# Two linear-attention branches under a gate: x^T phi(k) partial products carried on in PSUM, and some min-and-epsilon steps on GpSimd

## The chip, the cores and the metric

The kernel runs on one core of one Trainium2 chip. The metric is the device time of one execution in microseconds (us), from runs on the chip; the median of the runs shown is compared. "PE" is TensorE, "PEld" its weight loads, "DVE" VectorE, "ACT" ScalarE, "POOL" GpSimd.

## The reference

Two branches, A and B, work on the same input x (2048 rows of 640, bf16) with their own weights, and a sigmoid gate mixes their outputs:

```
phi(t) = where(t > 0, t + 1, exp(t)) + 1e-6
q, k, v = x @ wqkv                       # 32 heads of 20
kv  = phi(k)^T v        z = sum over rows of phi(k)
o   = phi(q) kv / (phi(q) z + 1e-6)
branch = o @ wo
out = g * A(x) + (1 - g) * B(x),   g = sigmoid(sum(x * gate_w))
```

## The kernel before, in words

The kernel never makes v. It uses phi(k)^T v = (x^T phi(k))^T wv, so that the long product over 2048 rows is G = x^T phi(k), 640 x 640, and everything behind it is small until the output product. The order of the work on TensorE, for branch A and then for branch B:

- **k chunks** (`k_chunk`, matmuls L205). x is cut into 16 chunks of 128 rows. A chunk is ten matmuls of 320 columns into one PSUM slot of two banks; there are four slots, `ps0` to `ps3`, used in turn. `phi` then makes phi(k) from the slot in three steps: ScalarE writes e = exp(slot) to SBUF (L195), VectorE makes e = min(e, 1) + epsilon (L198), and VectorE makes pk = max(slot + 1 + epsilon, e) (L202), which reads the slot a last time and so frees it. The tile `e` has three buffers.
- **q units** (`q_unit`, `q_block`, L254 and L265): the same for phi(q), transposed, with 1024 columns for a `phi`.
- **z** (`z_rows` L370, `z_pass` L385): column sums of phi(k), and `zsel`, with which the denominators are made.
- **G, last fifth** (`g_pass`, L288): the fifth column block of x against all of pk, into slot 1; ScalarE copies it out (L285).
- **G, the other four fifths** (`g_strassen`, products `g_prod` L315): a 2 x 2 block product by Strassen's method in Winograd's form, seven products of 16 matmuls of 320 columns in place of eight. The sums of blocks that it needs are made earlier by VectorE (`x_sum`, `k_sum`, by `add_rows` L454). The accumulators are `even` (slot 0) and `odd` (slot 1). The first product, P1, is needed in several results: ScalarE copies it to an SBUF tile `p1` in fp32 (L337), and VectorE adds `p1` to three later products while it takes them out of PSUM (`add`, L332).
- **the denominators** (`rec_pass` L435: 40 matmuls L169 into slot 2, then twice an L444 and a reciprocal L449 on VectorE), **their spreading** (`norm_spread`: eight matmuls L491 into slots 2 and 3, two ScalarE copies L496 to `R`), and **scaling** (`scale` L504, five VectorE products of 2048 columns on phi(q)). These stand between the products of `g_strassen`.

In branch B, `p_diff` (four L454 of 1280 columns) stands behind k chunks 3, 6, 9 and 12. After B's `g_strassen` the output stage begins: `kvt_mm` (L396), `kvt_mask` (L403) and so on, and then the output product, again by Strassen's method, in pairs of row blocks.

The order on each engine is the order of the program text wherever `tc.manual_schedule()` holds: in the first chunks of A, and from A's chunk 14 to the end. Between them (A's chunks 4 to 13 and five q pieces) the framework orders the work itself. `hc` is 8.

Of the kernel before, what the change touches and what calls it, by code (L numbers as in the profile page):

```python
# [12 lines left out]
ALU = mybir.AluOpType  # L13
# [8 lines left out]
HF = D // 2  # L22
# [3 lines left out]
EPS = 1e-6  # L26
# [5 lines left out]
def kernel(  # L32
# [11 lines left out]
    nc = tc.nc  # L44
# [19 lines left out]
    def ps(name, slot=None):  # L64

        return ps_raw(name, slot).bitcast(FP32).rearrange("p (b n) -> p b n", b=2)
# [3 lines left out]
    pk = persist.tile([P, ST, D], BF16, name="pk")  # L70
# [14 lines left out]
    hc, ic = ST // 2, 2 * P  # L85

    def flat(t, pattern, inner, at=0):
        n = hc * inner
        return t[:].rearrange(pattern)[:, at * n:(at + 1) * n].rearrange("p (i n) -> p i n", i=hc)

    S3 = persist.tile([P, 3, hc, ic], BF16, name="S3")
    SX = {k: S3[:, k - 1] for k in (1, 2, 3)}
    SX[4] = flat(M[1], "p c d -> p (c d)", ic)
    TK = [{k: flat(pqT[1], "p c s -> p (c s)", HF, k - 1) for k in (1, 2, 3, 4)},
          {k: flat(xT, "p c s -> p (c s)", HF, k - 2) for k in (2, 3, 4)}]
# [33 lines left out]
    for n in range(1, NB):  # L129
        for c in range(DT):  # L130
            nc.sync.dma_start_transpose(
                out=xT[:, c, n * HB:(n + 1) * HB], in_=x2[n * HB:(n + 1) * HB, c * P:(c + 1) * P]
# [4 lines left out]
    for r in range(4):  # L137
# [3 lines left out]
        out=spread[:].rearrange("p (h t) -> p h t", t=TW), in_=I4[:, :, None].to_broadcast([P, H, TW])  # L141
    )
    nc.gpsimd.memset(maskE[:], 1.0)
    for sign, base in ((1, 0), (-1, Dh - 1)):
        nc.gpsimd.affine_select(
            out=maskE[:], in_=maskE[:], pattern=[[-sign * Dh, KG // Dh], [0, Dh]],
# [3 lines left out]
    for r in range(4):  # L150
        rows = slice(32 * r, 32 * r + 32)
        for sign, base in ((1, 0), (-1, Dh - 1)):
            nc.gpsimd.affine_select(
                out=E4[rows], in_=E4[rows], pattern=[[sign, D]],
# [9 lines left out]
    def by_group(dst, lhsT, src, h):  # L164

        for c in range(DT):
            for j in range(4):
                r0 = h * 2 * HB + j * RB
                nc.tensor.matmul(  # L169
                    dst[32 * j:32 * j + 32, :], lhsT=lhsT[:, c, :], rhs=src[:, c, r0:r0 + RB],  # L170
                    start=(c == 0), stop=(c == DT - 1), tile_position=(0, 32 * j),
                )
# [16 lines left out]
        for lo, hi in zip(cuts, cuts[1:]):  # L189
            copy(out=xT[:, lo:hi, i * P:(i + 1) * P], in_=src[:, lo:hi])  # L190

    def phi(dst, src, n, lifted=False):

        e = work.tile([P, 2, n], BF16, tag="e", name="e", bufs=3)
        nc.scalar.activation(out=e[:], in_=src, func=ACT.Exp)  # L195
        if lifted:
            nc.scalar.activation(out=dst, in_=src, func=ACT.Identity, bias=lift[:])
        nc.vector.tensor_scalar(e[:], e[:], 1.0, EPS, op0=ALU.min, op1=ALU.add)  # L198
        if lifted:
            nc.vector.tensor_tensor(out=dst, in0=dst, in1=e[:], op=ALU.max)  # L200
            return
        nc.vector.scalar_tensor_tensor(out=dst, in0=src, scalar=1.0 + EPS, in1=e[:], op0=ALU.add, op1=ALU.max)  # L202
# [5 lines left out]
        )  # L208

    def k_done(b, i, pt):  # L210
        phi(pk[:, i, :].rearrange("p (b n) -> p b n", b=2), pt[:, :, 0:HF], HF)

    def k_chunk(b, i, slot=None):
        pt = ps(f"k{'AB'[b]}", slot)
        for hf in range(2):
            for c in range(DT):
                k_mm(b, i, c, pt, hf)
        k_done(b, i, pt)
# [74 lines left out]
    def x_sum(k):  # L293

        x11, x21 = [xn[:, 0:hc, n:n + ic] for n in (0, ic)]
        x12, x22 = [xn[:, hc:ST, n:n + ic] for n in (0, ic)]
        a, b, op = {
            1: (x21, x22, ALU.add), 2: (SX[1], x11, ALU.subtract),
            3: (x11, x21, ALU.subtract), 4: (x12, SX[2], ALU.subtract),
        }[k]  # L300
        add_rows(SX[k], a, b, op)

    def k_sum(b, k):

        b11, b12 = [pk[:, 0:hc, n * HF:(n + 1) * HF] for n in range(2)]
        b21, b22 = [pk[:, hc:ST, n * HF:(n + 1) * HF] for n in range(2)]
        t = TK[b]
        left, right = {1: lambda: (b12, b11), 2: lambda: (b22, t[1]), 3: lambda: (b22, b12), 4: lambda: (b21, t[2])}[k]()
        add_rows(t[k], left, right, ALU.subtract)

    def g_prod(pt, left, right, first):

        for i in range(hc):
            for n in range(2):
                nc.tensor.matmul(  # L315
                    pt[:, n, 0:HF], lhsT=left[:, i, n * P:(n + 1) * P], rhs=right[:, i, :],
                    start=(first and i == 0), stop=(i == hc - 1), skip_group_check=not first,
                )

    def g_strassen(b, norm):  # L320

        x11, x12 = [xn[:, k:k + hc, 0:ic] for k in (0, hc)]
        x22 = xn[:, hc:ST, ic:2 * ic]
        b11 = pk[:, 0:hc, 0:HF]
        b21, b22 = [pk[:, hc:ST, n * HF:(n + 1) * HF] for n in range(2)]
        lo, hi = GT

        def temp(name):
            return work.tile([P, 2, HF], FP32, tag="osb", name=name, bufs=3)

        def add(dst, pt, sb):
            nc.vector.tensor_tensor(out=dst, in0=pt[:, :, 0:HF], in1=sb[:], op=ALU.add)  # L332

        even, odd = ps("gs0", 0), ps("gs1", 1)
        g_prod(even, x11, b11, True)
        p1 = temp("p1")
        nc.scalar.copy(out=p1[:], in_=even[:, :, 0:HF])  # L337
        g_prod(odd, SX[2], TK[b][2], True)
        u2 = temp("u2")
        add(u2[:], odd, p1)  # L340
        k_sum(b, 4)
        norm()
        g_prod(even, x12, b21, False)
        nc.scalar.copy(out=lo[:, 0:2, :], in_=even[:, :, 0:HF])
        scale(b, 0)
        if b == 0:
            x_sum(4)
        g_prod(odd, SX[3], TK[b][3], False)
        u3 = temp("u3")
        add(u3[:], odd, p1)  # L350
        scale(b, 1)
        scale(b, 2)
        even = ps("gs0", 0)
        g_prod(even, SX[1], TK[b][1], True)
        add(hi[:, 2:4, :], even, u3)
        scale(b, 3)
        g_prod(odd, x22, TK[b][4], False)
        add(lo[:, 2:4, :], odd, p1)
        scale(b, 4)
        g_prod(even, SX[4], b22, False)  # L360
        for n in range(2):
            nc.vector.tensor_tensor(out=hi[:, n, :], in0=even[:, n, 0:HF], in1=u2[:, n], op=ALU.add)
# [72 lines left out]
    def rec_pass(b, zsel, slot):  # L435

        pt = ps(f"den{'AB'[b]}", slot)
        for h in range(2):
            by_group(pt[:, 0, h * RB:(h + 1) * RB], zsel, pqT[b], h)
        rts = []  # L440
        for h in range(2):
            part = slice(h * RB, (h + 1) * RB)
            d1 = work.tile([P, RB], FP32, tag="d1", name="d1")
            nc.vector.scalar_tensor_tensor(  # L444
                out=d1[:], in0=pt[:, 0, part], scalar=EPS, in1=ge[b][:, part], op0=ALU.add, op1=ALU.mult
            )
            rT = work.tile([P, RB], BF16, tag="rT", name="rT")
            with nc.allow_low_precision(reason="a fp32 reciprocal, stored as the bf16 that multiplies bf16"):
                nc.vector.reciprocal(out=rT[:], in_=d1[:])  # L449
            rts.append(rT)  # L450
        return rts

    def add_rows(dst, a, b, op):
        nc.vector.tensor_tensor(out=dst, in0=a, in1=b, op=op)  # L454
# [30 lines left out]
    def norm_spread(b, rts, slots):  # L485

        pts = [ps(f"ex{'AB'[b]}", s) for s in slots]
        for h in range(2):
            for j in range(4):
                rows = slice(32 * j, 32 * j + 32)  # L490
                nc.tensor.matmul(  # L491
                    pts[j // 2][:, j % 2, h * RB:(h + 1) * RB], lhsT=spread[rows, :], rhs=rts[h][rows, :],
                    start=True, stop=True,
                )
        for jj in range(2):
            nc.scalar.copy(  # L496
                out=R[:, :, 2 * jj:2 * jj + 2, :].rearrange("p h j n -> p j h n"),
                in_=pts[jj][:].rearrange("p j (h n) -> p j h n", n=RB),
            )

    def scale(b, m):

        rec = R[:].rearrange("p h j n -> p (h j n)")
        nc.vector.tensor_tensor(out=pqT[b][:, m, :], in0=pqT[b][:, m, :], in1=rec, op=ALU.mult)  # L504
# [127 lines left out]
    def g_all(b, zsel):  # L632

        g_pass(b, DT - 1, 1)
        k_sum(b, 3)
        rts = rec_pass(b, zsel, 2)
        g_strassen(b, lambda: norm_spread(b, rts, (2, 3)))


    with tc.manual_schedule():  # L640
# [12 lines left out]
    for n in range(1, NB):  # L653
        nc.sync.dma_start(
            out=xn[:, n * CB:(n + 1) * CB, :], in_=x2[n * HB:(n + 1) * HB, :].rearrange("(q p) d -> p q d", p=P)
# [11 lines left out]
    with tc.manual_schedule():  # L667
# [5 lines left out]
        zsel = q_pass(0, [(m, 1) for m in range(DT)])  # L673
        wq[1] = load_w(1, "q", nc.sync)
        g_all(0, zsel)

        turn[0] = 3
# [10 lines left out]
        zsel = q_pass(1, [(m, h) for h in range(2) for m in range(DT)])  # L688
# [53 lines left out]
        for i in range(1, half):  # L742
            p, after = pairs[i], pairs[i + 1] if i + 1 < half else None
# [53 lines left out]
```

## Time and profile before

| | |
|---|---|
| median of 2 runs | 192.75 us (192.75 to 192.76) |
| profiled execution, span from first to last instruction | 190.2 us |
| the difference of the two | 2.55 us |
| mean granted TensorE clock | 0.997 |
| PE busy in 27 to 38 us (A's k chunks 8 to 15) | 11.00 of 11.00 us |
| PE busy in 74.2 to 96.2 us (B's k chunks) | 22.00 of 22.00 us; DVE 18.67, ACT 10.56, POOL 0.00 |
| PE busy in 122.6 to 137 us (B's G) | 14.40 of 14.40 us; DVE 13.16 |
| PE busy in 137 to 147 us (end of B's G, begin of the output) | 9.85 of 10.00 us; DVE 8.56 |
| POOL, whole span | 8.5 us busy, all before 10 us |

The profile is of one execution; its own time is given only as the span. The span does not hold what lies before the first and after the last instruction; the difference to the median stands in the table. A line of the timeline reads: start, duration, engine, source line, operation, output and inputs with their shapes, and how many instructions were merged. A line of the chain of waits reads: start, duration, engine, tile, source line.

### The profile page before, as it was taken

The page shows a single profiled execution, that of the slowest core. Times are in us where ns is not written, and L with a number is a line of the kernel's source. Part 1 is how long each engine was busy: PE and PEld are TensorE (multiplying, and loading weights), DVE is VectorE, ACT ScalarE, POOL GpSimd, SP SyncE. Part 2 cuts the span into 40 slices and gives each one's busy share as a digit, 9 for nine tenths or more (in the row PEclk, how much of TensorE's full clock was granted, in tenths as well). Part 3 has the DMA queues.
Part 4 walks back from the last instruction along what each step waited for, and adds up shares of the span by engine and source line. Part 5 has one row for each costly group of instructions (what it writes and reads, how often), then busy time and mean ns, then how long its engine had stood idle before and what let it go on. Part 6 is the DMA issues. An engine that isn't in the chain of part 4 may idle for free.

```text
span 190.2 us, 3774 instructions
## 1 busy us (share of the span) xinstructions
PE 185.8 (98%) x1575; PEld 125.4 (66%) x1575; DVE 151.6 (80%) x242; ACT 70.0 (37%) x98; POOL 8.5 (4%) x23
## 2 busy tenths in 40 slices
PE   8999999999999999999999999999999999999992
PEld 3766657765576777777765555576777776777772
DVE  1498779898989997799976785899797989787553
ACT  2155445455941502355543654511501611111110
POOL 8900000000000000000000000000000000000000
PEclk9999999999999999999999999999999999999998
DMA  6965459970050000500000007000000002312112
GB/s 194 332 147 89 101 117 374 281 201 3 2 172 3 0 0 0 150 26 0 3 0 0 3 2 172 3 0 0 3 0 0 3 0 97 113 69 72 69 69 71
DMA packets 18880, 14.00 MB, mean 74 GB/s; under 512 B 9392, under 2 KB 18864, under 8 KB 18864
## 3 DMA queue, kind: packets, MB, share of 16 engines
q1 hardware_dynamic: 18288, 13.11, 25.0%
q10 hardware_dynamic: 576, 0.66, 1.0%
q8 instruction: 12, 0.20, 0.5%
q14 instruction: 4, 0.03, 0.1%
HBM read 9.18 MB, written 2.62 MB: 62 GB/s over the span
## 4 chain that ended last, share of the span: by engine, by line
PE 92%; DVE 5%; issue 1%; ACT 0%; DVEq 0%; ACTq 0%
PE gs L315 13%; PE qB L254 12%; PE kA L205 12%; PE kB L205 11%; PE qA L254 7%; PE ox L515 5%; PE oy L515 5%; PE oz L515 5%; PE qA L265 5%; PE ow L515 2%; PE gB L288 2%; PE gA L288 2%; DVE pqTB L504 2%; PE warm L162 2%; PE mA L429 2%; DVE osb L520 1%
## 5 line engine op out<-in xcount | busy, mean ns | idle before, releaser
L205 PEld LDWEIGHTS <-xT 128*128 128x128 bf16 x320 | 31.0, 98 | 12.4 <-DVE xT L190 0.2
L198 DVE TENSOR_SCALAR e<-e 128x640 bf16<-128x640 bf16 (+1 forms) x52 | 18.9, 363 | 11.6 <-ACT e L195 11.1
L205 PE MATMUL kA<-wkA,xT 128*128 128x320 bf16 x160 | 22.6, 299 | 0.0
L254 PE MATMUL qB<-xT,wqB 128*128 128x512 bf16 x100 | 22.5, 380 | 0.0
L205 PE MATMUL kB<-wkB,xT 128*128 128x320 bf16 x160 | 22.1, 299 | 0.0
L195 ACT ACTIVATE e<-kB 128x640 bf16<-128x640 f32 x16 | 11.3, 704 | 20.7 <-PE kB L205 19.4
L254 PEld LDWEIGHTS <-wqB 128*128 128x128 bf16 x100 | 11.4, 118 | 9.7 <-issue 0.7
L195 ACT ACTIVATE e<-kA 128x640 bf16<-128x640 f32 x16 | 11.1, 704 | 12.5 <-PE kA L205 12.5
L195 ACT ACTIVATE e<-qB 128x1024 bf16<-128x1024 f32 x10 | 10.2, 1023 | 12.7 <-PE qB L254 12.7
L202 DVE SCALAR_TENSOR_TENSOR pk<-kA,e 128x640 bf16<-128x640 f32 x16 | 13.2, 825 | 1.7
L202 DVE SCALAR_TENSOR_TENSOR pk<-kB,e 128x640 bf16<-128x640 f32 x16 | 13.2, 824 | 1.7
L195 ACT ACTIVATE e<-qA 128x1024 bf16<-128x1024 f32 x10 | 10.2, 1023 | 10.6 <-PE qA L254 5.2
L254 PE MATMUL qA<-xT,wqA 128*128 128x512 bf16 x60 | 13.6, 380 | 0.0
L202 DVE SCALAR_TENSOR_TENSOR pqTB<-qB,e 128x1024 bf16<-128x1024 f32 x10 | 12.2, 1224 | 1.0
L315 PEld LDWEIGHTS <-xn 128*128 128x128 bf16 x96 | 9.1, 98 | 4.2 <-issue 0.8
L315 PEld LDWEIGHTS <-S 128*128 128x128 bf16 x96 | 9.4, 98 | 3.6
L558 ACT COPY u<-ox 128x320 f32<-128x320 f32 x8 | 3.4, 425 | 21.9 <-PE ox L515 21.9
L254 PEld LDWEIGHTS <-wqA 128*128 128x128 bf16 x60 | 6.9, 118 | 5.6 <-issue 0.3
L515 PEld LDWEIGHTS <-xT 128*128 128x128 bf16 x85 | 8.0, 98 | 3.1 <-DVE xT L454 0.2
L515 PEld LDWEIGHTS <-pqTA 128*128 128x128 bf16 x85 | 7.9, 98 | 2.9 <-issue 0.2
L515 PEld LDWEIGHTS <-pqTB 128*128 128x128 bf16 x80 | 7.8, 98 | 3.0
L542 ACT COPY p1s<-ox 128x320 f32<-128x320 f32 x8 | 3.4, 426 | 16.8 <-PE ox L515 16.8
(120 smaller groups left out, 288.1 us busy)
## 6 DMA issues: line engine op xcount, KB each, us to landing
out_dram<-osb SPq DMA_DIRECT2D x14, 160.0 KB, 1.8
xn<-in_A_x_dram SPq DMA_DIRECT2D x3, 640.0 KB, 6.3
wqA<-in_A_wqkv_dram SPq DMA_DIRECT2D x1, 800.0 KB, 5.5
wvA<-in_A_wqkv_dram SPq DMA_DIRECT2D x1, 800.0 KB, 9.6
woA<-in_A_wo_dram SPq DMA_DIRECT2D x1, 800.0 KB, 12.6
wkB<-in_B_wqkv_dram SPq DMA_DIRECT2D x1, 800.0 KB, 4.7
wqB<-in_B_wqkv_dram SPq DMA_DIRECT2D x1, 800.0 KB, 4.8
wvB<-in_B_wqkv_dram SPq DMA_DIRECT2D x1, 800.0 KB, 4.6
```

Of the source, the lines that this page charges most:

```text
L162: nc.tensor.matmul(warm[:, 0, :], lhsT=one_l, rhs=one_r, start=True, stop=True)
L195: nc.scalar.activation(out=e[:], in_=src, func=ACT.Exp)
L198: nc.vector.tensor_scalar(e[:], e[:], 1.0, EPS, op0=ALU.min, op1=ALU.add)
L202: nc.vector.scalar_tensor_tensor(out=dst, in0=src, scalar=1.0 + EPS, in1=e[:], op0=ALU.add, op1=ALU.max)
L205: nc.tensor.matmul(pt[:, hf, 0:HF], lhsT=xT[:, c, i * P:(i + 1) * P], rhs=wk[b][:, c, hf * HF:(hf + 1) * HF], start=(c == 0), stop=(c == D ...
L254: nc.tensor.matmul(pt[:, u, :], lhsT=mixed(wq[b][:, c, :], m), rhs=xT[:, c, n * HB:(n + 1) * HB], start=(c == 0), stop=(c == DT - 1),)
L265: nc.tensor.matmul(pt[:, u, :], lhsT=mixed(wq[b][:, c, :], m + u), rhs=xT[:, c, n * HB:(n + 1) * HB], start=(c == 0), stop=(c == DT - 1),)
L288: nc.tensor.matmul(pt[:, hf, 0:HF], lhsT=xn[:, i, c * P:(c + 1) * P], rhs=pk[:, i, hf * HF:(hf + 1) * HF], start=(i == 0), stop=(i == ST - 1),
L315: nc.tensor.matmul(pt[:, n, 0:HF], lhsT=left[:, i, n * P:(n + 1) * P], rhs=right[:, i, :], start=(first and i == 0), stop=(i == hc - 1), s ...
L429: nc.tensor.matmul(dst[32 * g:32 * g + 32, :], lhsT=mixed(heads, c), rhs=wo_sb[b][:KG, 2 * g + k, hf * HF:(hf + 1) * HF], start=(k == 0), ...
L504: nc.vector.tensor_tensor(out=pqT[b][:, m, :], in0=pqT[b][:, m, :], in1=rec, op=ALU.mult)
L515: nc.tensor.matmul(dst, lhsT=left[:, c, r0:r0 + P], rhs=right[:, c, :], start=(first and c == 0), stop=(c == DT - 1), skip_group_check=not ...
```

## The change

It has two parts.

In `g_strassen`, P1's copy no longer goes to SBUF: ScalarE copies it from `even` to `odd` in PSUM, and the second product is accumulated onto it. `odd` then holds P1 + P2, later P1 + P2 + P4, and later that plus P6, so that three results come out by a plain ScalarE copy in place of a VectorE addition with `p1`. `rec_pass` moves from ahead of `g_strassen` to between the first product and the second; `norm_spread` moves from behind the second product to behind the third (in branch A behind `x_sum(4)` in the text, which is VectorE's); the five `scale` calls move back by some places.

In `phi` the step e = min(e, 1) + epsilon can be given to another engine. `k_done` gives it to GpSimd for chunks with i % 3 == 1, in branch A only those beyond `hc`: A's chunks 10 and 13, B's chunks 1, 4, 7, 10 and 13, seven in all.

```diff
-    def phi(dst, src, n, lifted=False):
+    def phi(dst, src, n, lifted=False, eng=None):
...
-        nc.vector.tensor_scalar(e[:], e[:], 1.0, EPS, op0=ALU.min, op1=ALU.add)
+        (eng or nc.vector).tensor_scalar(e[:], e[:], 1.0, EPS, op0=ALU.min, op1=ALU.add)
...
     def k_done(b, i, pt):
-        phi(pk[:, i, :].rearrange("p (b n) -> p b n", b=2), pt[:, :, 0:HF], HF)
+        eng = nc.gpsimd if i % 3 == 1 and (b == 1 or i > hc) else None
+        phi(pk[:, i, :].rearrange("p (b n) -> p b n", b=2), pt[:, :, 0:HF], HF, eng=eng)
...
         even, odd = ps("gs0", 0), ps("gs1", 1)
         g_prod(even, x11, b11, True)
-        p1 = temp("p1")
-        nc.scalar.copy(out=p1[:], in_=even[:, :, 0:HF])
-        g_prod(odd, SX[2], TK[b][2], True)
+        nc.scalar.copy(out=odd[:, :, 0:HF], in_=even[:, :, 0:HF])
+        rts = rec_pass(b, zsel, 2)
+        g_prod(odd, SX[2], TK[b][2], False)
         u2 = temp("u2")
-        add(u2[:], odd, p1)
+        nc.scalar.copy(out=u2[:], in_=odd[:, :, 0:HF])
         k_sum(b, 4)
-        norm()
         g_prod(even, x12, b21, False)
         nc.scalar.copy(out=lo[:, 0:2, :], in_=even[:, :, 0:HF])
-        scale(b, 0)
         if b == 0:
             x_sum(4)
+        norm_spread(b, rts, (2, 3))
         g_prod(odd, SX[3], TK[b][3], False)
         u3 = temp("u3")
-        add(u3[:], odd, p1)
+        nc.scalar.copy(out=u3[:], in_=odd[:, :, 0:HF])
+        scale(b, 0)
         scale(b, 1)
-        scale(b, 2)
         even = ps("gs0", 0)
         g_prod(even, SX[1], TK[b][1], True)
         add(hi[:, 2:4, :], even, u3)
+        scale(b, 2)
         scale(b, 3)
         g_prod(odd, x22, TK[b][4], False)
-        add(lo[:, 2:4, :], odd, p1)
+        nc.scalar.copy(out=lo[:, 2:4, :], in_=odd[:, :, 0:HF])
         scale(b, 4)
         g_prod(even, SX[4], b22, False)
```

`g_all` calls `g_strassen(b, zsel)` and no longer `rec_pass`. Below, P1 to P7 are the products in the order of the text.

More of the change, by code (lines that the diff above doesn't have):

```diff
@@ L318, in g_prod, with g_strassen @@
                 )
-    def g_strassen(b, norm):
+    def g_strassen(b, zsel):
         x11, x12 = [xn[:, k:k + hc, 0:ic] for k in (0, hc)]
@@ L635, in g_all @@
         k_sum(b, 3)
-        rts = rec_pass(b, zsel, 2)
-        g_strassen(b, lambda: norm_spread(b, rts, (2, 3)))
+        g_strassen(b, zsel)
     with tc.manual_schedule():
```

## The prediction

> **What bounds the kernel now.** I read the page's busy times and slices first, then the chain of waits, then the timeline of the two stages that the change touches.
>
> ```profile
> PE 185.8 (98%) x1575; PEld 125.4 (66%) x1575; DVE 151.6 (80%) x242; ACT 70.0 (37%) x98; POOL 8.5 (4%) x23
> PE   8999999999999999999999999999999999999992
> PEclk9999999999999999999999999999999999999998
> ```
>
> TensorE is at work in every slice but the first and the last, at full clock; the change leaves the number and size of its matmuls as they are. So the question of a few us is not what VectorE saves, but where TensorE waits for anybody. The chain of waits goes along TensorE from 0.84 to 137.40 us and from 145.50 to 184.08; in between it leaves it once:
>
> ```profile
> 132.60 0.33 PE exB L491 x8
> 132.93 4.47 PE gs L315 x32
> ...
> 143.12 1.13 DVE pqTB L504
> 144.25 0.80 DVE GT L362 x2
> 145.05 0.41 DVE KVT L403
> 145.45 0.04 issue
> 145.50 0.93 PE mid L396 x20
> ```
>
> VectorE is late with the scaling and the additions at the end of branch B's G, and TensorE waits for the mask of L403. How long, the timeline shows: the matmuls before it (L515, from 144.50, five at 0.136) leave room from 145.18, so the wait is 145.50 - 145.18 = 0.32 us. The waits for single engines show TensorE waiting otherwise only 0.8 us at the start. Nothing else in the part that changes can be won.
>
> **The change, part 1: G, branch B** (A has the same order, one `x_sum` of 1.22 more on VectorE, and no reader that is pressed behind it; its second group of k chunks follows).
>
> ```profile
> 128.09 2.35 PE L315 MATMUL gs<-pk,xn 128*128 128x320 bf16 x16
> 130.47 0.69 ACT L337 COPY p<-gs 128x640 f32<-128x640 f32 x1 [2.68 <-PE gs L315]
> 133.02 1.93 ACT L496 CAST R<-exB 128x1024 bf16<-128x1024 f32 x2 [1.86 <-PE exB L491]
> 134.98 1.23 DVE L504 TENSOR_TENSOR pqTB<-pqTB,R 128x2048 bf16<-128x2048 bf16 x1
> 141.57 2.34 PE L315 MATMUL gs<-pk,MB 128*128 128x320 bf16 x16
> 144.17 0.88 DVE L362 TENSOR_TENSOR GT<-gs,u 128x320 bf16<-128x320 f32 x2
> ```
>
> The rows to use: a product takes 2.18 us of TensorE (its record is 0.16 longer, as the ends overlap), the denominators' 40 matmuls 1.21, the spreading 0.33, an ACT copy of 640 columns 0.69, `R` 1.93, a scaling 1.12 from start to start, an addition (L332) 0.74.
>
> Removed from VectorE: three additions per branch, 6 in all, 6 x 0.74 = 4.4 us, of which 2.2 in B. Added to ScalarE: u2, u3 and half of lo, 3 x 0.69 per branch; it is idle for most of this stage. The copy of P1 stays one copy of 0.69.
>
> *The new wait.* P2 must wait for the copy from `even` to `odd`. TensorE now goes from L288 straight to P1 (126.88 to a record end of 129.23), the copy runs from 129.26, 0.03 behind as before, to 129.95, and the 40 matmuls of the denominators, which TensorE does in the meantime, end near 130.28. The copy has 1.0 us and needs 0.7, so the wait costs nothing. No row shows ScalarE writing PSUM. The bounds: the 0.43 that it takes for 320 columns (a gain of nothing, as the cover is larger anyway) and 1.38, twice the row, which would cost 1.38 - 1.0 = 0.4 per branch, 0.8 in all. I take 0.69: same engine, same source, same 640 columns.
>
> *The denominators.* They end at 130.34 in place of 128.15. VectorE needs 4.27 us from there to its second reciprocal (128.20 to 132.48 before); TensorE before had P1 and P2 to cover it, 4.37, and now has P2 and P3, the same 4.37. So the spreading starts at 134.8 without a new wait.
>
> *The scaling comes later.* ScalarE first copies lo (P3 ends at 134.75, so 134.95 to 135.6), then makes `R`: 135.6 to 137.5. Before, `R` was ready at 134.95; that is 2.5 us later. VectorE is free by then (the reciprocal ends at 134.7, `k_sum(4)` at 136.2). From there: scalings 0 and 1 from 137.5 to 139.75; P5's addition (L332 into `hi`; P4 ends at 137.3, P5 at 139.5, so it does not wait) to 140.5; scalings 2, 3 and 4 to 143.86. Before, scaling 4 ended at 144.25. The 2.2 us saved and the 2.5 us lost nearly cancel: before, VectorE had room between 136.2 and 137.4, which is now filled. The two additions of L362 then wait for P7, whose record ends at 143.91: they start at 143.94 in place of 144.17, 0.23 earlier, and with them the mask and L396. The gain is 0.23 of the 0.32 us. In detail it hangs on differences of a tenth; I take 0.2, with 0 (scalings 0.4 later than I have them) and 0.32 (the whole wait) as ends.
>
> The other queues: u3 is copied behind `R` (137.5 to 138.2) and must be out before P6 goes into `odd` at 139.5: 1.3 us to spare. The addition into hi ends at 140.5, before P7 is written to `even` at 141.65. P1 itself starts 1.2 us earlier, into slot 0, whose last reader (a q unit, L202) ended at 125.44. In A all of this shifts TensorE by nothing, and the k chunks behind it do not read what is late.
>
> **Part 2: GpSimd's steps.** Saved on VectorE: seven starts of 0.42, 2.9 us, in stages where TensorE is full (22.00 of 22.00 us in B's). That is worth nothing. The cost is a longer way from exp to pk:
>
> ```profile
> 93.48 0.71 ACT L195 ACTIVATE e<-kB 128x640 bf16<-128x640 f32 x1 [0.65 <-PE kB L205]
> ...
> 94.47 0.82 DVE L454 TENSOR_TENSOR D<-pqTA 128x1280 bf16<-128x1280 bf16 x1
> 95.20 0.32 DVE L198 TENSOR_SCALAR e<-e 128x640 bf16<-128x640 bf16 x1
> 95.63 0.82 DVE L202 SCALAR_TENSOR_TENSOR pk<-kB,e 128x640 bf16<-128x640 f32 x1
> ```
>
> This is B's chunk 13, the tightest. Chunks come every 1.36 us, four slots turn, so L202 must end 4.0 us after its exp began; here it ends 2.97 after, 1.05 to spare. The `e` buffers, three, give the same limit. With a GpSimd step of length P, L202 can start 0.70 + 0.05 + P + 0.05 after exp's start and ends 0.82 later: 1.62 + P. TensorE waits only if P exceeds 2.4 us. What is queued behind the waiting L202 on VectorE is the next chunk's L198; per three chunks VectorE has 3 x 0.74 + 2 x 0.42 + 0.73 = 3.79 us of work in 4.08, so it catches up. Behind chunk 15, z's last matmuls want pk near 99.2; it is there at 98.77, and at 97.39 + P where GpSimd sets the pace, so P to 1.8 is free there too. In A chunks 10 and 13 have more room.
>
> P has no row. GpSimd's nearest are these, and VectorE's own beside them:
>
> ```profile
> L153 POOL TENSOR_SCALAR_AFFINE_SELECT E<-E 32x640 bf16<-32x640 bf16 x8 | 5.7, 712 | 0.4
> L198 DVE TENSOR_SCALAR e<-e 128x640 bf16<-128x640 bf16 x32 | 10.4, 325 | 3.1 <-ACT e L195 2.6
> ```
>
> The lower end is 0.33, the upper 1.42 (twice the select, as there are two operations). I take 0.8, near the select of the same 640 columns. At every value between, TensorE waits for nothing: 0 us. A step of 3 us would cost 0.6 for each of B's five and A's chunk 10, 3.6 us.
>
> One thing could eat the room: chunks 4, 7, 10 and 13 come just behind `p_diff`, which runs on VectorE when GpSimd would start (81.81 to 82.62, exp 4 ends at 81.96). If GpSimd had to wait for its end, L202 of chunk 4 would end at 83.54 + P in place of 82.88 + P, and the limit for P falls from 2.4 to 1.7; still above 1.42. No row of before shows the two engines together. In the Trainium skill, SBUF — State Buffer, § Who interferes with whom, GpSimd and a VectorE instruction with two SBUF inputs take a shared pair of ports by a lock, and the later one is fully blocked; by that rule the lower limit holds and the sum stays 0. For the limit of 1.7 I give the slow GpSimd 0.09 below and not 0.06.
>
> **The sum.** -0.2 (part 1, end of B) + 0 (copy) + 0 (part 2) = -0.2 us on the span, 190.2 to 190.0. The profile gives no other time of its execution than this span; the median of the two runs lies 2.55 above it, which I leave as it is: 192.55.
>
> **The rivals.**
>
> - *The scaling eats the saving.* `R` a few tenths later than I have it, and L396 waits as before or 0.3 longer: 192.75 to 193.05. For it: my margin is 0.1 to 0.4 us in a chain of nine pieces. Against it: nothing that the rows show.
> - *The copy into PSUM is slow.* From 1.0 us per copy on, P2 waits; at 1.38 us the time is 192.55 + 0.8 = 193.35. For it: no row. Against it: ScalarE's copies of 640 columns are all at 0.69 to 0.74.
> - *GpSimd is slow: slower than before.* From P = 2.4 (1.7 if it must wait for `p_diff`) TensorE runs out of slots six times. At P = 3 that is 3.6 us: 196.2; at P = 2.5 with the wait, 0.8 x 5 = 4.0: 196.6. For it: no row of this operation. Against it: 712 ns for the select.
> - *VectorE's 7.3 us saved count.* That would be 192.75 - 7.3 = 185.4. Against it: TensorE is full; the one wait is 0.32 us. What is left is at most 192.4.
>
> **How the numbers follow.** Forecast (192.3 to 192.7): 0.62. Scaling eats the saving (192.7 to 193.1): 0.18. Slow copy (193.1 to 193.7): 0.07. Slow GpSimd (193.7 to 197): 0.09. Faster than 192.3: 0.04. To leave out no more than 2 in 10 the range goes from 192.3 to 193.5; it leaves out the slow GpSimd, the fastest case and the worst copies. Against 2% (3.86 us), about what a measurement of this kernel can tell from no change, only GpSimd at 3 us or so would count as slower: 0.04; faster 0.01; same 0.95.
>
> **What would show it.** Right: L169 between P1 and P2 without a gap in PE behind it; L396's second group at 145.2 to 145.3; GpSimd's seven steps at 0.5 to 1.4 us; PE still at 22 of 22 us in B's k chunks. Wrong: a gap in PE before P2 (the copy), before the spreading (the denominators), or in the chunk after a GpSimd step, with ACT or PE waiting for DVE L202.

## The result and the profile after

The changed kernel takes 195.28 us (median of 2 runs, 195.10 to 195.47) against 192.75: 2.5 us more by the medians; ratio 1.0136, 95% interval 1.0095 to 1.0177. Its profiled execution took 195.10 us with a span of 193.4. The page's busy times, its group of GpSimd's new steps (the last numbers: busy us, mean ns of one, then the idle time before them), and the waits (in total, times, longest):

```profile
PE 186.6 (96%) x1567; PEld 125.3 (65%) x1575; DVE 146.0 (75%) x229; ACT 73.9 (38%) x104; POOL 24.9 (13%) x30
```

```profile
L198 POOL TENSOR_SCALAR e<-e 128x640 bf16<-128x640 bf16 x7 | 16.4, 2345 | 73.4 <-ACT e L195 73.4
```

```profile
DVE pk L202 <- POOL e L198: 5.7, 3, 2.6
PE kA L205 <- DVE pk L202: 1.6, 1, 1.6
PE zB L371 <- DVE pk L202: 0.4, 1, 0.4
```

VectorE is 5.6 us less busy, and the kernel is slower: a GpSimd step takes 2.35 us, three times the 0.8 that I had taken, and TensorE, which waited for nobody in these stages before, now waits for L202. (In the changed kernel the lines behind `k_done` have moved by one number: L315 is now L316, L396 is L397, L504 is L505; the copy of P1 is L337 in both. In the runs further down they have moved by up to five.)

Where the time went is read from TensorE's starts. The span also holds the first loads, and with them the start of TensorE's second group of k matmuls moves between 15.2 and 17.0 us in these profiles, whatever the kernel. So I measure from that group on, in one profile of each kernel: to the L288 of branch A (stage A), from there to the L288 of B (stage B), and on to the second group of L396 (end of G). Times in us, each the difference of two starts in a timeline, beside the measured ratio to the kernel before:

| kernel | stage A | stage B | end of G | sum against before | ratio (95% interval) |
|---|---|---|---|---|---|
| before | 36.19 | 71.01 | 23.06 | | |
| whole change | 38.20 | 72.23 | 22.84 | +3.01 | 1.0136 (1.0095 to 1.0177) |
| g_only | 36.18 | 71.01 | 22.85 | -0.22 | 0.9983 (0.9968 to 0.9997) |
| pool_only | 38.19 | 72.23 | 23.06 | +3.22 | 1.0158 (1.0131 to 1.0185) |
| g_poolA | 38.22 | 71.01 | 22.85 | +1.82 | 1.0096 (1.0068 to 1.0123) |
| g_poolB | 36.18 | 72.25 | 22.84 | +1.01 | 1.0049 (1.0033 to 1.0064) |
| g_poolA10 | 37.82 | 71.01 | 22.84 | +1.41 | 1.0109 (1.0061 to 1.0156) |
| g_poolA13 | 37.80 | 71.00 | 22.85 | +1.39 | 1.0109 (1.0053 to 1.0165) |
| poolA10_shift | 37.42 | 71.01 | 22.85 | +1.02 | 1.0091 (1.0059 to 1.0122) |
| poolA_noskip | 37.07 | 71.01 | 22.84 | +0.66 | 1.0034 (1.0012 to 1.0056) |
| half_step | 36.64 | 71.42 | 22.84 | +0.64 | 1.0016 (0.9994 to 1.0038) |
| one_op | 37.29 | 71.24 | 22.85 | +1.12 | 1.0031 (0.9994 to 1.0067) |
| idle_pool | 36.19 | 74.75 | 22.84 | +3.52 | 1.0169 (1.0132 to 1.0206) |
| g_poolB_no13 | 36.19 | 72.25 | 22.84 | +1.02 | 1.0047 (1.0032 to 1.0061) |
| poolB_late_diff | 36.19 | 72.17 | 22.84 | +0.94 | 1.0038 (1.0016 to 1.0060) |
| no_cover | 36.19 | 71.97 | 23.82 | +1.72 | 1.0104 (1.0070 to 1.0139) |

The rows of the table repeat to some 0.03 us between kernels that share a stage, so they tell apart what the ratios cannot. The sum of the whole change, 3.0 us, lies inside its interval of 1.8 to 3.4; so do the others in theirs, but for poolA10_shift, whose 1.02 us (0.53%) are a little under its interval.

Part 1 did what it should. The timeline of the whole change at the copy and at the end of B's G (start, duration, engine, line, operation):

```profile
132.76 1.28 PE L169 MATMUL denB<-pqTB,zsel 128*32 128x256 bf16 x40
132.93 0.68 ACT L337 COPY gs<-gs 128x640 f32<-128x640 f32 x1 [1.47 <-PE gs L316]
133.97 2.35 PE L316 MATMUL gs<-xT,S 128*128 128x320 bf16 x16
...
145.28 2.34 PE L316 MATMUL gs<-pk,MB 128*128 128x320 bf16 x16
147.66 0.89 DVE L363 TENSOR_TENSOR GT<-gs,u 128x320 bf16<-128x320 f32 x2
148.99 0.93 PE L397 MATMUL mid<-GT,wvB 128*80 128x80 bf16 x20
```

The copy into PSUM takes 0.68 us and ends at 133.61, the denominators go on to 133.97, and P2 follows at once. The additions begin 0.04 behind the record end of P7 (147.62), and L397's second group comes 22.84 us behind L288 in place of 23.06. It was close: the last scaling's record ends at 147.61.

Part 2 lost it. Stage A in the chain of waits (start, duration, engine, tile, line):

```profile
32.78 2.35 POOL e L198
...
35.16 0.82 DVE pk L202
...
37.82 0.45 issue
38.27 0.84 DVE pk L202
...
39.15 1.52 PE kA L205 x10
```

Chunk 10's L202 waits for GpSimd, everything behind it on VectorE shifts by 2.2 us, and TensorE stands before chunk 15 until L202 of chunk 12 is out. Why chunk 12 and not 11: a line ahead of chunk 15, `turn[0] = (turn[0] + 1) % 4`, skips a PSUM slot. Chunk 15 and the two pieces of work behind it therefore take the slot of the third piece of work ahead of them, not of the fourth.

Stage B loses 0.51 in the k chunks (from the first L205 of B to the first L254), 0.60 at z and 0.11 behind it. Its timeline:

```profile
87.89 0.70 ACT L195 ACTIVATE e<-kB 128x640 bf16<-128x640 f32 x1 [0.66 <-PE kB L205]
88.68 2.35 POOL L198 TENSOR_SCALAR e<-e 128x640 bf16<-128x640 bf16 x1 [1.74 <-ACT e L195]
88.88 0.70 DVE L198 TENSOR_SCALAR e<-e 128x640 bf16<-128x640 bf16 x1
...
90.42 0.81 DVE L455 TENSOR_TENSOR D<-pqTA 128x1280 bf16<-128x1280 bf16 x1
91.15 0.82 DVE L202 SCALAR_TENSOR_TENSOR pk<-kB,e 128x640 bf16<-128x640 f32 x1
```

This is chunk 7: L202 ends at 91.97, 4.08 us behind the start of its exp. That is more than four slots allow, and they allow less than the 4.0 of the prediction. In the timeline of the kernel before, the exp of B's chunk 12 and the q unit that takes its slot:

```profile
92.12 0.70 ACT L195 ACTIVATE e<-kB 128x640 bf16<-128x640 f32 x1 [0.65 <-PE kB L205]
...
96.00 2.32 PE L254 MATMUL qB<-xT,wqB 128*128 128x512 bf16 x10
```

TensorE comes back to a slot 3.88 us behind the start of its exp, and needs L202's end 0.04 before that (39.11 to 39.15 in the chain above), so L202 has 3.84. By the starts of the exps, the chunks that follow GpSimd's in their slots come 0.06 to 0.16 us late each. And VectorE's own step of chunk 6, begun 0.2 us behind GpSimd's, takes 0.70 in place of 0.32.

### The profile page after: what moved, and what is told of

The parts are those of the page before. It is cut to its first block, busy times and chain, and to the rows that moved or that the text cites. A ratio compares the mean times of both kernels' runs of the same rounds, so it can differ in the third digit from the quotient of the medians.

```text
span 193.4 us, 3757 instructions
## 1 busy us (share of the span) xinstructions
PE 186.6 (96%) x1567; PEld 125.3 (65%) x1575; DVE 146.0 (75%) x229; ACT 73.9 (38%) x104; POOL 24.9 (13%) x30
## 4 chain that ended last, share of the span: by engine, by line
PE 80%; DVE 11%; POOL 2%; DMA 2%; issue 1%; ACT 1%; ACTq 0%; DVEq 0%; POOLq 0%
PE gs L316 16%; PE qB L255 10%; PE kA L205 8%; PE qA L255 7%; DVE pk L202 6%; PE ox L516 6%; PE oy L516 5%; PE oz L516 5%; PE qA L266 4%; PE kB L205 4%; PE ow L516 2%; POOL e L198 2%; DMA xn<-in_A_x_dram 2%; PE gB L289 2%; PE gA L289 2%; DVE e L198 2%
## 5 line engine op out<-in xcount | busy, mean ns | idle before, releaser
L205 PEld LDWEIGHTS <-xT 128*128 128x128 bf16 x320 | 31.0, 98 | 15.0 <-issue 2.3
L198 DVE TENSOR_SCALAR e<-e 128x640 bf16<-128x640 bf16 (+1 forms) x45 | 18.1, 402 | 10.5 <-ACT e L195 10.5
L198 POOL TENSOR_SCALAR e<-e 128x640 bf16<-128x640 bf16 x7 | 16.4, 2345 | 73.4 <-ACT e L195 73.4
L205 PE MATMUL kA<-wkA,xT 128*128 128x320 bf16 x160 | 22.9, 299 | 1.8 <-DVE pk L202 1.6
L205 PE MATMUL kB<-wkB,xT 128*128 128x320 bf16 x160 | 22.5, 299 | 0.0
L202 DVE SCALAR_TENSOR_TENSOR pk<-kB,e 128x640 bf16<-128x640 f32 x16 | 13.2, 824 | 4.7 <-POOL e L198 3.5
L202 DVE SCALAR_TENSOR_TENSOR pk<-kA,e 128x640 bf16<-128x640 f32 x16 | 13.2, 825 | 4.2 <-POOL e L198 2.2
L202 DVE SCALAR_TENSOR_TENSOR pqTB<-qB,e 128x1024 bf16<-128x1024 f32 x10 | 12.2, 1225 | 1.0
L316 PEld LDWEIGHTS <-S 128*128 128x128 bf16 x96 | 9.1, 98 | 4.2 <-issue 0.8
L316 PEld LDWEIGHTS <-xn 128*128 128x128 bf16 x96 | 9.4, 98 | 3.6
```

What stands on the lines that cost most here:

```text
L198: (eng or nc.vector).tensor_scalar(e[:], e[:], 1.0, EPS, op0=ALU.min, op1=ALU.add)
L205: nc.tensor.matmul(pt[:, hf, 0:HF], lhsT=xT[:, c, i * P:(i + 1) * P], rhs=wk[b][:, c, hf * HF:(hf + 1) * HF], start=(c == 0), stop=(c == D ...
L316: nc.tensor.matmul(pt[:, n, 0:HF], lhsT=left[:, i, n * P:(n + 1) * P], rhs=right[:, i, :], start=(first and i == 0), stop=(i == hc - 1), s ...
```

## The experiments

The theory after the result: GpSimd's step is too long, part 1 is as forecast. The rivals: part 1 costs some of the loss; the hand-over between the engines costs, not the length; the two engines slow each other.

**The two parts alone, and the branches alone.** g_only has `eng = None` in `k_done`; pool_only is the kernel before with the change of `phi` and `k_done`.

```diff
 g_poolA
-        eng = nc.gpsimd if i % 3 == 1 and (b == 1 or i > hc) else None
+        eng = nc.gpsimd if b == 0 and i in (10, 13) else None
 g_poolB
+        eng = nc.gpsimd if b == 1 and i % 3 == 1 else None
```

Expected of g_only: 

> Part 1 alone, all steps on VectorE. Theory (the GpSimd steps cost everything, part 1 gains its quarter of a us at L397): 192.75 - 0.23 = 192.5, PE's second group of L397 about 0.2 us earlier than before, no gap ahead of the second product. Rival (the copy in PSUM or the later denominators cost some of the 2.5 us): above 193.

Expected of pool_only: 

> Part 2 alone. Theory: about 0.2 us slower than the whole change, 195.3 to 195.8, with TensorE losing 2.0 us in A's second group of k chunks, 0.5 in B's k chunks and 0.7 before the end of z in B. Rival (part 1 costs some of it): 194.5 or less.

Expected of g_poolA: 

> Part 1 and GpSimd for A's chunks 10 and 13 alone. Theory: 192.5 + 2.0 = 194.5. Rival (GpSimd's five steps in B are the greater part, being five of seven): 193.2 or less.

Expected of g_poolB: 

> Part 1 and GpSimd for B's chunks 1, 4, 7, 10 and 13 alone. Theory: 192.5 + 0.5 (k chunks) + 0.7 (z) = 193.7. Rival (B's loss came from entering late from A): 192.5 to 193.0.

Measured, against 192.28 us for the kernel before on that chip (the expectations start from 192.75): 192.10, 195.52, 194.51 and 193.37 us, that is -0.18, +3.24, +2.23 and +1.09. All four go with the theory and against the rivals; pool_only's is 0.2 above its range on that base. The stages add up without a rest: A's two steps 2.0 us, B's five 1.2, part 1 -0.22, whichever is combined with which. g_only is faster than the kernel before by 0.33 us at the ratio, interval 0.06 to 0.6.

**Which of A's two steps, and the slot.** `i in (10, 13)` becomes `i == 10` or `i == 13`; poolA_noskip drops one line.

```diff
 poolA_noskip (on g_poolA)
         k_chunk(0, ST - 2)
-        turn[0] = (turn[0] + 1) % 4
```

Expected of g_poolA10: 

> Part 1 and GpSimd for A's chunk 10 alone. Theory (chunk 15 has the slot of chunk 12, three chunks earlier and not four, as one slot is skipped ahead of it; VectorE, held for 2.35 us by chunk 10, frees it too late): PE waits 0.15 us before chunk 14 and about 0.6 before chunk 15, ratio to before about 1.003 (-0.2 + 0.75 us). Rival (each of A's two steps costs its half of 2.0 us): ratio 1.004 and more, 0.8 + us in both single runs.

Expected of g_poolA13: 

> Part 1 and GpSimd for A's chunk 13 alone. Theory: no wait before chunk 15, as chunk 12's slot is free in time; VectorE is late with chunks 14 and 15 and the gate's matmuls L169 begin 0.3 to 0.6 us late: ratio to before about 1.001 to 1.002. Rival: 0.8 us or more lost before chunk 15.

Expected of poolA_noskip: 

> GpSimd for A's chunks 10 and 13 with part 1, without the line that skips a slot ahead of chunk 15, which then follows chunk 11 in its slot. Theory (the skipped slot makes A's loss): the wait of 1.6 us before chunk 15 goes, 0.2 to 0.6 us of A's loss stay; ratio to before 1.000 to 1.003, against 1.0096 with the skip. Rival (A's loss is VectorE being late as such): the loss comes back behind the next slots, ratio 1.007 or more.

Chunk 10 alone costs 1.63 us, chunk 13 alone 1.61, and both together 2.0. My numbers for the single steps were misses (0.75 and 0.3 to 0.6): each is as dear as nearly both. In g_poolA13 the wait is at a place that I had not expected, in its timeline:

```profile
37.59 2.35 POOL L198 TENSOR_SCALAR e<-e 128x640 bf16<-128x640 bf16 x1 [27.90 <-ACT e L195]
39.97 0.82 DVE L202 SCALAR_TENSOR_TENSOR pk<-kA,e 128x640 bf16<-128x640 f32 x1 [2.63 <-POOL e L198]
40.84 2.32 PE L255 MATMUL qA<-xT,wqA 128*128 128x512 bf16 x9 [1.46 <-DVE pk L202]
```

The q unit behind chunk 15 takes chunk 13's slot, so that slot too is used again by the third piece of work behind it. In the kernel before, that q unit starts 2.52 us behind the exp of chunk 13 (35.50 to 38.02), so chunk 13 may take 2.5 us from exp to the end of L202, not 4.0: it takes 4.1 (36.71, its exp, to 40.79), and the 1.6 too much is what A loses. Without the skip the same two steps lose 0.89 us and not 2.04, more than the 0.2 to 0.6 that I expected; the wait before chunk 15 is gone and that of the q unit is 0.24. The slot made more than half of A's loss. In the rest VectorE is late behind GpSimd, and 0.46 us of unexplained idle time ahead of chunk 12's L202 stand on that chain too (see below). The kernel without the skip and without GpSimd's steps was not run.

**Half of the step, and one operation of it.**

```diff
 half_step
-        (eng or nc.vector).tensor_scalar(e[:], e[:], 1.0, EPS, op0=ALU.min, op1=ALU.add)
+            eng.tensor_scalar(e[:, 0], e[:, 0], 1.0, EPS, op0=ALU.min, op1=ALU.add)
+            nc.vector.tensor_scalar(e[:, 1], e[:, 1], 1.0, EPS, op0=ALU.min, op1=ALU.add)
 one_op (epsilon left out of e in the seven chunks)
+            eng.tensor_scalar(e[:], e[:], 1.0, None, op0=ALU.min)
```

Expected of half_step: 

> The whole change, but GpSimd makes 320 of the 640 columns and VectorE the other 320. Theory (the length of the step is what costs, not the hand-over): the step takes 1.2 us, B's k chunks and z lose nothing, A's 0.3 or less; ratio to before 0.998 to 1.001. Rival (a fixed cost of each hand-over between the engines): the step still takes 2 us or the time stays 1.5 us or more above before.

Expected of one_op: 

> The whole change, but GpSimd's step does the min alone and leaves epsilon out of e in those seven chunks. Theory (GpSimd's time goes with operations per element): the step takes about 0.2 + 1.1 = 1.3 us in place of 2.35, and the time is near half_step's. Rival (it goes with elements moved and converted): 2.2 to 2.35 us as with two operations, and the time stays that of the whole change.

The groups of GpSimd's steps in half_step and in one_op:

```profile
L201 POOL TENSOR_SCALAR e<-e 128x320 bf16<-128x320 bf16 x7 | 9.4, 1340 | 77.4 <-ACT e L195 77.4
```

```profile
L201 POOL TENSOR_SCALAR e<-e 128x640 bf16<-128x640 bf16 x7 | 12.6, 1804 | 76.0 <-ACT e L195 76.0
```

Half the columns take 1.28 us (the mean holds one of 1.72 that began within p_diff), so by these two sizes a step costs about 0.2 us and 3.3 ns a column, (2.35 - 1.28) / 320. One operation takes 1.80: the second costs 0.54 us, 0.85 ns a column. Both my ends for one_op were wrong. The loss follows the length: A's from 2.0 to 0.45 (half; 0.3 or less expected) and 1.1 us (one operation), and B's k chunks lose nothing in either. In half_step chunk 13's L202 ends 2.92 us behind its exp (35.97 to 38.89), 0.4 over its 2.5. But z still loses 0.3 in half_step, where I expected nothing, and length alone does not explain that.

**Contention.** idle_pool gives all steps of phi back to VectorE and lets GpSimd do seven of the same kind that nobody waits for.

```diff
 idle_pool (on g_only)
+        if i % 3 == 1 and (b == 1 or i > hc):
+            nc.gpsimd.tensor_scalar(M[0][:, 0, :], pk[:, i - 1, :], 1.0, EPS, op0=ALU.min, op1=ALU.add)
```

Expected of idle_pool: 

> Part 1, every step of phi on VectorE, and seven GpSimd instructions of the same kind and size that read the chunk of pk before and write to a tile that is not in use, so that nothing waits for them. Theory (what costs is that L202 waits for GpSimd): ratio 0.998 to 1.001, though L198 is stretched by up to 0.4 us where it starts just behind a GpSimd step. Rival (what costs is that GpSimd and VectorE slow each other): 0.8 us or more lost in A or B, ratio 1.003 or more.

The rival won, in B: nothing lost in A (36.19), 3.74 us in B, more than the change itself loses there. (In the change VectorE is also rid of five steps in B; here it keeps them.) B's timeline:

```profile
83.51 0.81 DVE L457 TENSOR_TENSOR D<-pqTA 128x1280 bf16<-128x1280 bf16 x1
83.75 2.78 POOL L213 TENSOR_SCALAR MA<-pk 128x640 bf16<-128x640 bf16 x1 [3.13 <-DVE pk L202]
84.24 0.84 DVE L198 TENSOR_SCALAR e<-e 128x640 bf16<-128x640 bf16 x1
...
85.92 0.78 DVE L198 TENSOR_SCALAR e<-e 128x640 bf16<-128x640 bf16 x1
...
96.50 3.14 PE L205 MATMUL kB<-wkB,xT 128*128 128x320 bf16 x20 [0.73 <-DVE pk L202]
```

GpSimd, begun within p_diff, takes 0.43 longer, and two of VectorE's L198 take 0.84 and 0.78 in place of 0.32. VectorE had no room for 1.0 us in each three chunks: before, they already took it 3 x 1.16 + 0.73 = 4.2 us, against TensorE's 4.08. In idle_pool's A the L198 that overlap GpSimd's steps are at 0.32 to 0.33; in A of the whole change one that begins 0.2 behind a step takes 0.70 (37.07). So stretching is real; it hangs on where in GpSimd's step L198 falls.

**What makes z wait in B.** g_poolB_no13 has `i in (1, 4, 7, 10)`; poolB_late_diff moves the last p_diff of g_poolB from behind chunk 12 to behind chunk 15.

Expected of g_poolB_no13: 

> Part 1 and GpSimd for B's chunks 1, 4, 7 and 10, chunk 13 on VectorE. Theory (the wait at z comes from chunk 13's step, the last one before it, and VectorE catches up without it): z loses 0.2 us or less, the k chunks still their 0.5; ratio about 1.0016. Rival (VectorE is late from the steps before as well): z still loses 0.5 or more, ratio 1.004 or more.

Expected of poolB_late_diff: 

> As g_poolB (part 1 and GpSimd for B's five chunks), but the last of the four p_diff instructions stands behind chunk 15 and not behind chunk 12, so that VectorE has 0.73 us less to do ahead of z. Theory (z's 0.6 us are VectorE's backlog, as its three-chunk period has grown past TensorE's): z loses 0.1 us or less, the k chunks still 0.5. Rival (z waits for GpSimd's last step itself): z still loses 0.5 or more.

Both theories lost: z keeps 0.63 and 0.50 us (stage from the first L254 to the first L429: 3.98 and 3.85, against 3.35). Without chunk 13's step VectorE is late from the ones before. With less work for VectorE it waits for chunk 13's step, as the timeline of poolB_late_diff shows:

```profile
97.91 0.82 DVE L202 SCALAR_TENSOR_TENSOR pk<-kB,e 128x640 bf16<-128x640 f32 x1 [0.56 <-POOL e L198]
...
101.11 0.43 PE L371 MATMUL zB<-pk,ones 128*32 128x320 bf16 x5 [0.32 <-DVE pk L202]
```

So two limits lie at nearly the same place, VectorE's backlog and GpSimd's length, and taking away one shows the other. Both taken away at once was not tried, other than by g_only, which loses nothing.

**The 0.5 us that nothing explains.** In every kernel but the next in which GpSimd's step in A's chunk 10 takes 1.8 us or more, VectorE stands idle for 0.5 us before chunk 12's L202, 0.45 of it in the chain above as "issue". poolA10_shift adds a memset of a 128x1 tile (`nc.vector.memset(one1[:], 0.0)`) at the very beginning, which moves every later VectorE instruction by one place.

Expected of poolA10_shift: 

> As g_poolA10 with one more memset of a 128x1 tile on VectorE at the very beginning, which moves every later VectorE instruction by one place in its queue. Theory (the unexplained 0.5 us before chunk 12's L202 sits at a place in VectorE's instruction stream): the gap is before another instruction, and the loss in A falls from 1.63 towards 1.2 us. Rival (it belongs to chunk 12's L202): the gap stays before that instruction and the loss at 1.6.

The two L202 of chunk 12, in g_poolA10 and in poolA10_shift:

```profile
38.77 0.82 DVE L202 SCALAR_TENSOR_TENSOR pk<-kA,e 128x640 bf16<-128x640 f32 x1 [0.52 <-PE kA L205]
```

```profile
38.36 0.82 DVE L204 SCALAR_TENSOR_TENSOR pk<-kA,e 128x640 bf16<-128x640 f32 x1
```

The gap is gone and A's loss falls from 1.63 to 1.23, so 0.4 us of the loss was this gap. The theory had it come up before another instruction, and it did not. The run speaks for a place in VectorE's stream and against the work itself, but it is one kernel and one profile; what makes the gap stays open.

**The cover of the copy.** no_cover is g_only with `rec_pass` called ahead of `g_prod(even, x11, b11, True)`, so that P2 follows P1 directly.

Expected of no_cover: 

> Part 1 with the denominators' matmuls ahead of the first product, so that the second follows the first directly and the copy from even to odd has no cover; no GpSimd steps. Theory (the 40 matmuls hide the copy): PE waits 0.16 + 0.03 + 0.68 + 0.04 = 0.9 us before the second product in each branch, 1.8 us in all, ratio about 1.0077. Rival (something later in the stage ends last anyway): under 1 us, ratio 1.003 or less.

Measured 194.73 us against 192.73. TensorE waits in each branch, and both G stages are 0.97 us longer (22.27 against 21.31 from A's L288 to B's first L205; 23.82 against 22.85 in B). The waits:

```profile
PE gs L316 <- ACT gs L338: 1.6, 2, 0.8
```

The theory holds: 1.93 us in all where 1.8 was expected. The 40 matmuls hide a copy that would cost some 1 us per branch.

## Why the prediction was wrong, point by point

- **The likeliest case, 192.55 us, and the range to 193.5 were wrong; the rival that GpSimd is slow came true, at a lower P and in another place than it was priced.** I gave it 0.09 and left it out of the range.
- **The mis-sized term: P.** "I take 0.8, near the select of the same 640 columns", with 1.42 as the upper end. It is 2.35. The select at 712 ns was a row of another operation on a quarter of the partitions; doubling it was no bound. With no row of the operation itself the end should have been set by what would hurt (2.4 and 1.8 us, which the text had) and the range should have reached there.
- **The limit of 2.4 us for P** was 0.2 too high. L202 has 3.84 us from its exp's start, not 4.0. The hand-overs are 0.08 and 0.03 (chunk 4 in the whole change: 84.51 to 84.59, 86.94 to 86.97), 0.11 in all where I had 0.10. So P may be 3.84 - 1.63 = 2.2, and 2.35 is 0.15 too long: chunk 8, in chunk 4's slot, comes 0.16 late (its exp 1.52 behind that of chunk 7 in place of 1.36). From chunk 7 on L202 starts 0.12 behind GpSimd's end (91.03 to 91.15), as VectorE is then still in p_diff. These small delays add up to the 0.5 us in B's k chunks.
- **"so P to 1.8 is free there too"**, at z: right as a formula. At 2.35 it gives 0.55 us, and 0.60 was lost. But it named one limit of two; VectorE's backlog is the other (g_poolB_no13).
- **"In A chunks 10 and 13 have more room": the step that failed worst, 2.0 of the 3.2 us.** That four slots are used in turn holds only where `turn` is not moved by hand. The skipped slot leaves chunk 13 2.5 us in place of 4.0, and with it a P of some 0.85 us (2.5 less the 1.62 of my sum). Any P above that costs in A: my 0.8 would just have fitted, and my upper end of 1.42 would not. The term was put at 0 and is 2.0, of which about 0.4 may be the unexplained gap.
- **"it catches up"**, 3.79 us of VectorE's work in 4.08: wrong by the 0.38 to 0.44 by which one L198 in three chunks is stretched. From 91.15 to 95.38, L202 of chunk 7 to that of chunk 10, VectorE needs 4.23. I had asked whether GpSimd would be held up by p_diff, and not what it would do to L198.
- **The lock.** The trace of the whole change shows p_diff at its usual 0.82 within a GpSimd step (85.23 to 86.05 within 84.59 to 86.94). GpSimd was held back by 0.43 where p_diff came first (idle_pool). L198 ended 0.90 us behind GpSimd's start (88.68 and 89.58), which fits being held until some 0.58 into the step and then run in 0.32. In one_op a p_diff begun 0.16 behind a step's start (84.45 and 84.29) took 1.24, which gives the same 0.6. In the Trainium skill, SBUF — State Buffer, § Who interferes with whom, whoever issues first has the shared pair for the whole instruction and the other is fully blocked; here VectorE was blocked for the first 0.6 us of a step of 1.8 or 2.35. A p_diff begun later than that was not blocked at all, and L198 once more near a step's end (idle_pool).
- **Part 1: right.** -0.2 forecast, -0.22 in the stages of every kernel that has it as written, 0.9983 in the ratio. The copy (0.69 forecast, 0.68), the denominators without a new wait, P7's record end as what the additions wait for: as written. The rival that the scaling eats the saving did not come, though the scaling ended only 0.01 us ahead of P7's record.

## What to carry to other kernels

Where TensorE is full, work taken off an engine beside it is worth nothing, and a slower engine put into a chain that frees buffers is paid as soon as its step outlasts the slack; so work out that slack at every buffer, with the rotation as the code really turns it, a skipped slot included. If the moved operation has no row of its own, set its upper end by what it would have to be to hurt. An instruction that nobody waits for can still cost time, where it slows an engine that has no room left: 3.74 us in B of idle_pool.

## What had not been expected of the hardware

- GpSimd's two-operation step on 128x640 bf16 took 2.35 us, seven times VectorE's 0.33: by two sizes about 0.2 us and 3.3 ns a column, of which the second operation is 0.85.
- GpSimd and VectorE hold each other up for parts of an instruction: VectorE's L198 took 0.70 to 0.84 us in place of 0.32 where it began 0.1 to 0.5 behind the start of a GpSimd step or 0.6 before its end (85.92 in idle_pool, the step ending at 86.53), and its usual 0.32 in between (35.27 in idle_pool's A, within a step from 34.37 to 36.72) and 0.33 where it began 0.14 before the end (36.58, the same step). By the ends of the held instructions the hold at the start lasts about 0.6 us with 640 columns, of one operation or two, and 0.3 with 320 (half_step: 0.44 in place of 0.23, begun 0.11 behind the step's start). This is an estimate.
- A gap of 0.5 us in VectorE's stream went away when one instruction was added at the very beginning.
- ScalarE's copy of 128x640 fp32 from PSUM to PSUM took 0.68 us, against 0.69 to SBUF.
